# One head group of batch 1 transposed by DMA instead of TensorE

## The chip, the cores and the metric

The kernel runs on one core of a Trainium2 chip. The metric is the device time of one execution in microseconds (us); the time of a kernel is the median of its runs. A profile is one execution recorded instruction by instruction; its span runs from the first to the last instruction.

## What is computed

Attention with squared ReLU in place of a softmax, for 8 batches of 12 heads, 448 positions and head width 64, then a normalized two-layer feed-forward with a residual:

```
scores = q @ k.T / sqrt(64)
attn   = maximum(scores, 0)**2 / 448
x      = heads side by side of (attn @ v)          # 8 x 448 x 768
xn     = (x - mean) / sqrt(var + 1e-6) * g_ln
out    = x + maximum(xn @ w_ch1, 0) @ w_ch2        # 768 -> 3072 -> 768
```

## The kernel before, in words

The order of all work is written out by hand: each engine runs its instructions in the order in which the program emits them, and a helper, `interleave` (L13), deals the units of one list among those of another.

Attention goes by groups. A group is one batch and four heads (two pairs of heads); batch b has the groups 3b, 3b+1 and 3b+2, so group 5 is the third group of batch 1, and groups 6 to 8 belong to batch 2. For each group q, k and v are loaded by POOL's DMA queue with a cast to bf16 (`load`, L108). The scores contract over the head width, so q and k have to be transposed first. Two ways are in the kernel:

- `transposes` (L180): TensorE transposes 14 blocks of q and 14 of k against an identity (L201) into PSUM, and VectorE copies them to SBUF (L208). Used for batches 0 and 1 (`by_dma = 2`, L369).
- `keys_dma` and `queries_dma` (L224, L230): SyncE issues one DMA transpose for the keys (L228) and two for the queries (L233, L234). Used from batch 2 on.

The transposed keys by DMA go to three rotating buffers (`kT`), the transposed queries to two (`qT`). The same two are used by `transposes` for the first group of batch 1. The other groups of batch 1 have their transposes in `hold`, a buffer that also takes the raw q and k of batch 1; later the tile `xtok` lies in the same place.

`scores` (L273) multiplies, applies ReLU on ScalarE (L292) and squares on VectorE; `values` (L300) multiplies with v; `centre` (L349) subtracts the mean. For batches 0 and 1 attention is cut into two blocks of query positions (`attention_block`, L388), and the units of a block are dealt among the units of the first feed-forward product of the block before (`ffn1`, L487): the list at L595 to L611 is

```
interleave(ffn1_units(0, BLK[0][0]), attention_block(0, BLK[0][1]), 3, 1)
... second-layer weights, loads of groups 6 to 8 ...
interleave(ffn1_units(0, BLK[0][1]), attention_block(1, BLK[1][0]), 3, 1)
interleave(ffn1_units(1, BLK[1][0]), attention_block(1, BLK[1][1]), 3, 1)
tokens(0)
```

The transposes of group 5 are a unit of their own in the third of these lines. `tokens` (L463) is one long DMA transpose on SyncE (L467) that brings the attention output of a pair of batches to tokens on partitions; `statistics` (L471) and `roots` (L477) compute the scale of each token from it, and `ffn2` (L525) applies that scale to the second product. The scores of batch 2 and later are dealt among the units of `ffn2`.

On POOL's queue stand, in order: q, k, v of batch 0, the first-layer weights (`load_w1`, 12 DMAs), then q, k, v of group 3, q and k of group 4, q and k of group 5, v of groups 4 and 5 (each behind a product of batch 0), the second-layer weights (`load_w2`, 4 DMAs, L142), and q, k of groups 6, 7 and 8 with v of group 6. A DMA that reuses a buffer waits on that queue until the buffer's last reader is done.

Of the kernel before, what the change touches and what calls it, by code (L numbers as in the profile page):

```python
# [12 lines left out]
def interleave(main, side, free=0, ahead=0):  # L13


    for unit in side[:ahead]:
        unit()
    side = side[ahead:]
    n, done = len(main) - free, 0
    for i, unit in enumerate(main):  # L20
        unit()
        want = min(len(side), (len(side) * (i + 1)) // n)
        while done < want:
            side[done]()
            done += 1
# [3 lines left out]
def kernel(  # L29
# [23 lines left out]
    P = 128  # L53
# [8 lines left out]
    J = S // HP  # L62
    NP = H // 2
    G = NP // 2
# [35 lines left out]
    qkv = {}  # L100
# [5 lines left out]
    groups = [(b, m) for b in range(B) for m in range(G)]  # L106

    def load(n, names):  # L108
        if n >= len(groups):
            return  # L110
        b, m = groups[n]
        for name in names:
            if b == 1 and name != "v":
                o = (2 * m + "qk".index(name)) * 2 * S
                t = hold[:, o:o + 2 * S].rearrange("p (r s) -> p r s", r=2)
            elif name == "q":
                t = qbuf[m][:, D:D + 2 * S].rearrange("p (r s) -> p r s", r=2)
            else:
                t = io.tile([P, 2, S], bf16, tag=name, name=name + "_sb", bufs=4 if name == "v" else 3)
            nc.gpsimd.dma_start(t, srcs[name][b][:, m:NP:G, :])  # L120
            qkv[name, b, m] = t
# [8 lines left out]
    hold = xtpool.tile([P, K1, NT, P], bf16, tag="xtok", name="hold_sb")  # L130
    hold = hold.rearrange("p c t d -> p (c t d)")
# [3 lines left out]
    def load_w1(i):  # L135
        s = slice(i * NCH, (i + 1) * NCH)
        for hf in range(2):
            nc.gpsimd.dma_start(w1[hf * HP:(hf + 1) * HP, :, s], w1_src[hf][:, :, s])  # L138
# [11 lines left out]
    load(2, "v")  # L150
    for i in range(6):
        load_w1(i)
    load(3, "qkv")
    load(4, "qk")
    load(5, "qk")

    ones = const.tile([P, P], bf16)
    nc.vector.memset(ones, 1.0)
# [21 lines left out]
    def transposes(b, m):  # L180


        if b == 0:
            o = 12 * 1024 + m * 2 * J * P
            sb = early[:, o:o + 2 * J * P].rearrange("p (i c) -> p i c", c=P)
        elif m:
            o = (m - 1) * 2 * J * P
            sb = hold[:, o:o + 2 * J * P].rearrange("p (i c) -> p i c", c=P)
        else:
            sb = tpool.tile([P, NB, P], bf16, tag="qT", name="qT_sb")  # L190
        for i, n in enumerate(("q", "k")):
            src = qkv[n, b, m]
            if (b, m) == (0, 0):
                idle((36, 4)[i])
            if b == 0:
                ps = ps_mm.tile([P, 1024], bf16, tag="mm", name="tr_ps")
            else:
                ps = ps_sc.tile([P, 2, 1024], bf16, tag="sc", name="tr_ps")[:, 0]
            for j in range(J):
                for pr in range(2):  # L200
                    nc.tensor.transpose(  # L201
                        ps[pr * HP:(pr + 1) * HP, j * P:(j + 1) * P],
                        src[:, pr, j * D:(j + 1) * D], identity)

            cuts = ((nc.vector.tensor_copy, 0, 3), (nc.scalar.copy, 3, J)) if (b, n) == (0, "k") \
                else ((nc.vector.tensor_copy, 0, J),)
            for copy, lo, hi in cuts:
                copy(sb[:, i * J + lo:i * J + hi, :],  # L208
                     ps[:, lo * P:hi * P].rearrange("p (j c) -> p j c", c=P))
        if (b, m) == (0, 0):  # L210
            idle(3)
        squares_now()
        st[b, m] = {
            "q": lambda i, r: sb[:, 0:J],
            "k": lambda i: sb[:, J + i],
            "where": lambda pr, j: (j, pr),
            "attn": []}
# [6 lines left out]
    def keys_dma(n):  # L224
        if n >= len(groups):
            return
        kts[n] = tpool.tile([P, J, P], bf16, tag="kT", name="kT_sb", bufs=3)
        nc.sync.dma_start_transpose(kts[n], qkv[("k",) + groups[n]].rearrange("p r s -> p (r s)"))  # L228

    def queries_dma(n):  # L230
        m, kt = groups[n][1], kts[n]
        qt = tpool.tile([P, NB, P], bf16, tag="qT", name="qT_sb")
        nc.sync.dma_start_transpose(qt[:, 0:2 * J + 1:2, :], qbuf[m][:, :])  # L233
        nc.sync.dma_start_transpose(qt[:, 1:2 * J:2, :], qbuf[m][:, D:D + 2 * S])  # L234

        def queries(i, r):
            o = (2 * i + r) // J * J + 1 - r
            return qt[:, o:o + J]
        st[groups[n]] = {
            "q": queries,  # L240
            "k": lambda i: kt[:, i],
            "where": lambda pr, j: divmod(pr * J + j, 2),
            "attn": []}
# [122 lines left out]
                xc[b][:, c, of(blk)], total, g_mean[:, c:c + 1], xc[b][:, c, of(blk)],  # L366
                op0=ALU.mult, op1=ALU.add)

    by_dma = 2  # L369

    def transposed(n):

        if groups[n][0] < by_dma:
            transposes(*groups[n])
            return


        if n == by_dma * G:
            keys_dma(n)
        else:  # L380
            if n == by_dma * G + 1:
                load(n + 2, "k")
            load(n + 3, "k")
            load(n + 2, "q")
        queries_dma(n)
        keys_dma(n + 1)

    def attention_block(b, blk):  # L388


        lo, hi, first = b * G, b * G + G, blk[0] == 0
        units = [lambda: transposed(lo)] if first else []

        def unit(n, part):
            squares_now()
            for i in range(4 * part, min(4 * part + 4, J), 2):
                if (b, blk) == FIRST and n == G - 1:
                    busy(1)
                scores(n, tuple(range(i, min(i + 2, J))), blk)
            if b == 1 and not first and part and n == hi - 1:  # L400
                transposed(hi)
            if part and n > lo:
                values(n - 1, blk)
                if not first:
                    load(n + 3, "v")
        for n in range(lo, hi):
            units.append(lambda n=n: unit(n, 0))
            if first and n + 1 < hi:
                units.append(lambda n=n: transposed(n + 1))
            units.append(lambda n=n: unit(n, 1))  # L410

        def last():
            if (b, blk) == FIRST:
                busy(1)
            values(hi - 1, blk)
            if (b, blk) == FIRST:
                busy(2)
            if b == 1 and not first:
                load(hi + 3, "v")
        units.append(last)  # L420
        units.append(lambda: centre(b, blk))
        return units

    def attention(bs):

        lo, hi = bs[0] * G, (bs[-1] + 1) * G
        seq = [(n, i) for n in range(lo, hi) for i in range(J)]

        def item(n, i):
            if i == 0 and n + 1 < len(groups) and groups[n + 1][0] >= by_dma:
                transposed(n + 1)
            scores(n, (i,), FULL)

        def product(n):
            values(n, FULL)  # L440
            load(n + 4, "v")

        def bundle(items, at):
            for o, it in enumerate(items):
                item(*it)
                if o == at:
                    product(it[0] - 1)
        units, due = [], [[], []]
        for s in range(0, len(seq), 3):
            items = seq[s:s + 3]  # L450
            at = max((o for o, (n, i) in enumerate(items[:2]) if n > lo and i in (1, 2)), default=-1)
            units.append(lambda items=items, at=at: bundle(items, at))
            n = items[at][0] - 1
            due.append([groups[n][0]] if at >= 0 and groups[n][1] == G - 1 else [])
            units += [lambda b=b: centre(b, FULL) for b in due.pop(0)]
        units.append(lambda: product(hi - 1))
        units.append(lambda: None)
        return units
# [112 lines left out]
    def ffn1_units(b, blk=FULL):  # L571
        if blk == FULL:
            return [lambda ni=ni: ffn1(b, ni, blk) for ni in range(K2)]
        return [lambda: ffn1_head(b, blk)] + [lambda ni=ni: ffn1(b, ni, blk) for ni in range(3, K2)]
# [20 lines left out]
    pairs = B // 2  # L595
    for unit in attention_block(0, BLK[0][0]):
        unit()
    interleave(ffn1_units(0, BLK[0][0]), attention_block(0, BLK[0][1]), 3, 1)
    w2 = wpool.tile([P, K2, d_model], bf16, tag="w2", name="w2")
    for i in range(4):  # L600
# [52 lines left out]
```

## Time and profile before

| what | value |
|---|---|
| median of three runs | 551.65 us (550.57 to 553.97) |
| profiled execution, its own time | 549.99 us |
| its span | 548.2 us |
| granted TensorE clock | 0.997 |
| PE, DVE, ACT, POOL busy | 539.8, 266.3, 258.5, 110.4 us |
| transposes on TensorE (L201) for batch 1 | 84, from 42.1 to 54.7 us |
| first DMA transpose of keys and queries issued | 73.7 us |
| last second-layer weight DMA issued, landed after | 44.8 us, 26.7 us |

In the lines of the profile PE is TensorE's matmuls, PEld its weight loads, DVE VectorE, ACT ScalarE, POOL GpSimd and SP SyncE; a q behind the name (SPq) is the engine's queue, which issues DMAs. `L201` is line 201 of the kernel. In a timeline a line has the start, the duration, the instruction with what it writes and reads, how many were merged, and in brackets the idle time of the engine before it with what ended it. The row "DMA" of the forty slices gives the busy share of the DMA engines in tenths. Of the DMA queues, q0 (software_dynamic) carries what POOL issues and q1 (hardware_dynamic) what SyncE issues; the columns are packets, megabytes and the time of the packets as a share of the window.

### The profile page before, as it was taken

To read this page: it belongs to the slowest core of one execution; us is meant where nothing else is said; L and a number is where in the kernel's file an instruction comes from. 1 tells how busy PE (TensorE), PEld (TensorE's weight loads), DVE (VectorE), ACT (ScalarE), POOL (GpSimd) and SP (SyncE) were. 2 spreads that over 40 slices of the span, in tenths; PEclk is the share of its full clock that TensorE was granted. 3 is DMA by queue.
4 is the path that set the end of the run, shared out by engine and by line. 5 is a ranking of instruction groups with operands and counts; after the bars stand their busy time and mean duration, and the time that the engine had idled before them with its cause. 6 is when DMAs were issued, how large, how long until landed. Compare 5 with 4: busy or idle time off the path is not lost.

```text
span 548.2 us, 10993 instructions
## 1 busy us (share of the span) xinstructions
PE 539.8 (98%) x4742; PEld 319.0 (58%) x4742; DVE 266.3 (49%) x511; ACT 258.5 (47%) x420; POOL 110.4 (20%) x136
## 2 busy tenths in 40 slices
PE   7999999999999999999999999999999999999997
PEld 6687779755555555555555555555555555556665
DVE  3776753278887250057787532027687680001111
ACT  4676675555543444455545344445545254440000
POOL 8344102024424210002633400001230400000000
PEclk9899999999999999999999999999999999999999
DMA  9999999979994970018999892004941240001222
GB/s 144 206 205 208 211 190 172 111 116 158 148 179 92 155 112 1 0 41 131 159 157 143 108 155 35 0 1 92 169 102 30 59 102 0 1 0 30 59 57 59
DMA packets 107216, 56.16 MB, mean 102 GB/s; under 512 B 77216, under 2 KB 103712, under 8 KB 107168
## 3 DMA queue, kind: packets, MB, share of 16 engines
q0 software_dynamic: 27520, 25.96, 33.3%
q1 hardware_dynamic: 79408, 29.31, 31.8%
q8 instruction: 37, 0.61, 0.5%
q10 hardware_dynamic: 240, 0.20, 0.1%
q14 instruction: 11, 0.09, 0.0%
HBM read 51.91 MB, written 11.01 MB: 115 GB/s over the span
## 4 chain that ended last, share of the span: by engine, by line
PE 92%; DMA 5%; POOL 2%; issue 0%; DVE 0%; POOLq 0%
PE o_ps L533 39%; PE h_ps L495 38%; PE sc_ps L281 6%; PE av_ps L311 5%; DMA w<-in_moe_w_ch_dram 5%; PE o_ps L558 1%; PE h_ps L517 1%; PE sum_ps L359 1%; PE tr_ps L201 0%; POOL v_sb L120 0%; POOL k_sb L120 0%; POOL w L138 0%; POOL q_sb L120 0%; DVE o_sb L561 0%; POOL identity masks.py:199 0%
## 5 line engine op out<-in xcount | busy, mean ns | idle before, releaser
L495 PE MATMUL h_ps<-xc_sb,w 128*128 128x448 bf16 (+2 forms) x1368 | 219.1, 318 | 0.7 <-DVE hT_sb L501 0.4
L533 PE MATMUL o_ps<-w,hT_sb 128*128 128x384 bf16 x1296 | 219.6, 326 | 0.0
L495 PEld LDWEIGHTS <-w 128*128 128x128 bf16 x1368 | 128.6, 98 | 86.9 <-issue 3.2
L533 PEld LDWEIGHTS <-hT_sb 128*128 128x128 bf16 x1296 | 123.1, 98 | 94.3 <-issue 16.1
L292 ACT ACTIVATE attn_sb<-sc_ps 128x896 bf16<-128x896 f32 (+4 forms) x150 | 126.3, 902 | 83.6 <-PE sc_ps L281 83.6
L503 ACT ACTIVATE hT_sb<-h_ps 128x448 bf16<-128x448 f32 (+2 forms) x212 | 102.5, 483 | 121.6 <-PE h_ps L495 121.1
L294 DVE TENSOR_TENSOR attn_sb<-attn_sb 128x896 bf16<-128x896 bf16 x126 | 81.6, 654 | 38.1 <-ACT attn_sb L292 37.1
L539 DVE SCALAR_TENSOR_TENSOR o_sb<-o_ps,rstd_sb,xtok_sb 128x384 f32<-128x384 f32 x54 | 33.0, 611 | 48.5 <-PE o_ps L533 48.5
L480 DVE RECIPROCAL rstd_sb<-rstd_sb 128x1 f32<-128x1 f32 (+1 forms) x10 | 1.7, 168 | 97.5 <-ACT rstd_sb L479 97.5
L342 POOL TENSOR_TENSOR part_sb<-part_sb,xT_sb 128x448 f32<-128x448 f32 x24 | 29.5, 1229 | 70.5 <-DVE xT_sb L318 62.9
L474 DVE BATCH_NORM_STATS2 stats<-xtok_sb 128x6 f32<-128x384 bf16 x56 | 27.5, 533 | 33.3 <-DMA xtok_sb<-xT_sb 33.3
L365 DVE SCALAR_TENSOR_TENSOR xc_sb<-total_sb,g_mean,xc_sb 128x448 bf16<-128x448 f32 (+2 forms) x54 | 29.0, 606 | 21.3 <-ACT total_sb L363 21.3
L339 POOL TENSOR_TENSOR part_sb<-xT_sb 128x448 f32<-128x448 bf16 x6 | 6.6, 1105 | 140.1 <-DVE xT_sb L318 110.3
L281 PE MATMUL sc_ps<-qT_sb,kT_sb 64*64 64x448 bf16 x504 | 34.7, 357 | 0.0
L311 PE MATMUL av_ps<-attn_sb,v_sb 64*64 64x448 bf16 (+2 forms) x672 | 32.3, 327 | 0.0
L318 DVE TENSOR_SCALAR xT_sb<-av_ps 128x896 bf16<-128x896 f32 (+2 forms) x30 | 27.0, 901 | 10.4 <-PE av_ps L311 10.4
L311 PEld LDWEIGHTS <-v_sb 64*64 64x64 bf16 x840 | 23.3, 109 | 11.4 <-issue 2.5
L120 POOL DMA_DIRECT2D k_sb<-in_k_dram x21 | 15.1, 720 | 71.0 <-DMA kT_sb<-k_sb 38.5
L324 DVE TENSOR_SCALAR xc_sb<-xT_sb,g_sb 128x448 bf16<-128x448 bf16 (+2 forms) x58 | 28.8, 546 | 1.0
L120 POOL DMA_DIRECT2D v_sb<-in_v_dram x24 | 17.5, 733 | 21.6 <-PE av_ps L311 17.7
L281 PEld LDWEIGHTS <-kT_sb 64*64 64x64 bf16 x504 | 11.5, 105 | 16.9 <-issue 13.5
L292 ACT ACTIVATE early<-sc_ps 128x768 bf16<-128x768 f32 (+3 forms) x24 | 18.4, 826 | 1.5 <-PE sc_ps L281 1.3
(60 smaller groups left out, 195.6 us busy)
## 6 DMA issues: line engine op xcount, KB each, us to landing
out_dram<-o_sb SPq DMA_DIRECT2D x54, 192.0 KB, 2.9
v_sb<-in_v_dram POOLq DMA_DIRECT2D x24, 224.0 KB, 5.0
q_sb<-in_q_dram POOLq DMA_DIRECT2D x21, 224.0 KB, 7.5
k_sb<-in_k_dram POOLq DMA_DIRECT2D x21, 224.0 KB, 6.7
w<-in_moe_w_ch_dram POOLq DMA_DIRECT2D x12, 384.0 KB, 14.5
w<-in_moe_w_ch_dram POOLq DMA_DIRECT2D x4, 1152.0 KB, 20.0
hold_sb<-in_q_dram POOLq DMA_DIRECT2D x3, 224.0 KB, 11.9
hold_sb<-in_k_dram POOLq DMA_DIRECT2D x3, 224.0 KB, 11.2
```

What stands on the lines that cost most here:

```text
L120: nc.gpsimd.dma_start(t, srcs[name][b][:, m:NP:G, :])
L281: nc.tensor.matmul(ps[cols, r, o * w:(o + 1) * w], g["k"](i)[rows, cols], g["q"](i, r)[rows, blk[0]:sum(blk), cols], start=True, stop=True)
L292: nc.scalar.activation(a, ps[:, :, :len(slots) * w], ACTF.Relu)
L294: nc.vector.tensor_mul(a, a, a)
L311: nc.tensor.matmul(ps[cols, hh, :w], v_sb[rows, pr, j * D:(j + 1) * D], g["attn"][i][rows, r, :], start=(j == 0), stop=(j == J - 1))
L324: nc.vector.tensor_scalar_mul(xc[b][:, c, of(blk)], xT[b // 2][:, c, of(blk, b)], g_sb[:, c:c + 1])
L342: nc.gpsimd.tensor_add(part[b], part[b], x[:, c])
L365: nc.vector.scalar_tensor_tensor(xc[b][:, c, of(blk)], total, g_mean[:, c:c + 1], xc[b][:, c, of(blk)], op0=ALU.mult, op1=ALU.add)
L495: nc.tensor.matmul(ps[:, :w], w1[:, c, ni * P:(ni + 1) * P], xc[b][:, c, of(blk)], start=(c == 0), stop=(c == K1 - 1))
L503: nc.scalar.activation(hT[pair][:, ni, o:o + w], ps[:, :w], ACTF.Relu)
L533: nc.tensor.matmul(ps[:, :DH], hT[pair][:, ki, t * P:(t + 1) * P], w2[:, ki, cols], start=(ki == 0), stop=(ki == K2 - 1))
L539: nc.vector.scalar_tensor_tensor(o_sb[t][:, cols].rearrange("p (c d) -> p c d", d=D), ps[:, :DH].rearrange("p (c d) -> p c d", d=D), rstd[ ...
```

## The change

Group 5 is transposed by DMA. The border between the two ways is now counted in groups (`by_dma = 2 * G - 1`, which is 5, with G = 3 groups in a batch). Raw q of group 5 goes to the query buffer that group 2 used (`qbuf[2]`), raw k to one of the rotating k buffers. The loads of batch 1 are emitted after the first attention block, and those of group 5 stand right behind q and k of group 3, ahead of v of group 3 and q and k of group 4. The three DMA transposes of group 5 are the first on SyncE's queue after two small loads of `g_ln`. The transposed queries of group 5 take the first of the two `qT` buffers, those of group 3 the second; before, group 3 took the first and group 6 the second. `interleave` deals one unit fewer in that stage.

```
-            if b == 1 and name != "v":
+            if b == 1 and m < G - 1 and name != "v":
...
-    load(3, "qkv")
-    load(4, "qk")
-    load(5, "qk")
...
-            o = (m - 1) * 2 * J * P
-            sb = hold[:, o:o + 2 * J * P].rearrange("p (i c) -> p i c", c=P)
+            sb = hold[:, :2 * J * P].rearrange("p (i c) -> p i c", c=P)
...
-    by_dma = 2
+    by_dma = 2 * G - 1

     def transposed(n):
-        if groups[n][0] < by_dma:
+        if n < by_dma:
             transposes(*groups[n])
             return
-        if n == by_dma * G:
+        if n == by_dma:
+            keys_dma(n)
+            queries_dma(n)
+            return
+        if n == by_dma + 1:
             keys_dma(n)
         else:
-            if n == by_dma * G + 1:
+            if n == by_dma + 2:
                 load(n + 2, "k")
...
-            if first and n + 1 < hi:
+            if first and n + 1 < min(hi, by_dma):
                 units.append(lambda n=n: transposed(n + 1))
...
     for unit in attention_block(0, BLK[0][0]):
         unit()
+    load(3, "qk")
+    load(5, "qk")
+    transposed(by_dma)
+    load(3, "v")
+    load(4, "qk")
     interleave(ffn1_units(0, BLK[0][0]), attention_block(0, BLK[0][1]), 3, 1)
```

More of the change, by code (lines that the diff above doesn't have):

```diff
@@ L434, in item @@
         def item(n, i):
-            if i == 0 and n + 1 < len(groups) and groups[n + 1][0] >= by_dma:
+            if i == 0 and n + 1 < len(groups):
                 transposed(n + 1)
```

## The prediction

> **What bounds the kernel now.** I read the totals first, then the forty slices, the chain that ended last, the timeline of TensorE around the removed transposes, SyncE's timeline, the DMA queues by window, and last the moment at which the second pass of the feed-forward starts. The page of before:
>
> ```profile
> PE 539.8 (98%) x4742; PEld 319.0 (58%) x4742; DVE 266.3 (49%) x511; ACT 258.5 (47%) x420; POOL 110.4 (20%) x136
> ...
> DMA  9999999979994970018999892004941240001222
> ...
> PE 92%; DMA 5%; POOL 2%; issue 0%; DVE 0%; POOLq 0%
> ```
>
> TensorE is busy 98% and is 92% of the chain. But the DMA row stands at 9 in eleven of the first twelve slices (164 us) and at 7 in the other: in the stage that the change touches, two things are full, TensorE and the DMA engines. TensorE there (columns: start us, us, instruction):
>
> ```profile
> 52.50 1.48 PE L495 MATMUL h_ps<-xc_sb,w 128*128 128x256 bf16 x12
> 53.91 0.97 PE L201 MATMUL tr_ps<-identity,hold_sb 128*64 128x128 bf16 x28
> 54.82 1.49 PE L495 MATMUL h_ps<-xc_sb,w 128*128 128x256 bf16 x12
> ...
> 58.86 0.63 PE L281 MATMUL sc_ps<-hold_sb 64*64 64x256 bf16 x16
> ```
>
> No row has an idle time: what leaves TensorE here shortens the run, what makes it wait lengthens it. The 28 transposes of group 5 (batch 1, third group) begin at 53.91, the next work at 54.82. The scores of group 5 begin at 58.86. SyncE's DMA transposes and the DMA queues in 73.5 to 77.2 us and 77.2 to 80.6 us:
>
> ```profile
> 73.75 1.30 SPq L228 DMA_TRANSPOSE kT_sb<-k_sb  x1
> 75.16 2.07 SPq L233 DMA_TRANSPOSE qT_sb<-q_sb  x1
> 77.27 3.80 SPq L234 DMA_TRANSPOSE qT_sb<-q_sb  x1
> 81.11 1.30 SPq L228 DMA_TRANSPOSE kT_sb<-k_sb  x1
> 86.32 9.11 SPq L467 DMA_TRANSPOSE xtok_sb<-xT_sb  x1
> ```
> ```profile
> q0 software_dynamic: 887, 0.75, 126.3%
> ```
> ```profile
> q1 hardware_dynamic: 857, 0.22, 88.9%
> q0 software_dynamic: 265, 0.22, 44.4%
> ```
>
> q0 carries POOL's loads, q1 SyncE's transposes. The key transpose issued at 73.75 moved nothing before 77.2; it landed after 7.7 us, at 81.5, the two query transposes at 82.4 and 85.7. The first-pair token transpose (L467), issued at 86.32, landed 19.0 us later, and the second feed-forward product waits for it:
>
> ```profile
> 105.34 1.02 DVE L474 BATCH_NORM_STATS2 stats<-xtok_sb 128x6 f32<-128x384 bf16 x2 [15.24 <-DMA xtok_sb<-xT_sb]
> 106.64 0.29 ACT L479 ACTIVATE rstd_sb<-mv,eps_sb 128x1 f32<-128x1 f32 x1 [4.00 <-DVE mv L475]
> 106.84 2.51 ACT L292 ACTIVATE attn_sb<-sc_ps 128x896 bf16<-128x896 f32 x3
> 109.83 0.76 PE L281 MATMUL sc_ps<-qT_sb,kT_sb 64*64 64x448 bf16 x12
> ```
>
> ScalarE holds the square root and, behind it, the three evictions that free the three score accumulators. They end at 109.35; the third score of the next bundle needs its accumulator at 110.34 (two thirds into the 0.76 us from 109.83). The token transpose may land 1.0 us later than 105.3 before TensorE waits: at 106.3.
>
> **The change part by part.** The sum is made against the profiled execution: span 548.2 us, 549.99 us with what lies around it. The median of the three runs is 551.65, so 1.66 us are added at the end.
>
> *Removed.* 28 transposes with their weight loads: 54.82 - 53.91 = 0.91 us of TensorE, all on the path. Two VectorE copies at 0.616 us (the copy's own row): VectorE idles 1.44 us right after them, so they are worth nothing.
> By the Trainium skill (TensorE: Matmul & The Clock Gate, PE-mode transpose) a transpose costs about 275 ns in a kernel's context; 28 would be 7.7 us and the time 544. The row speaks against it: 28 in 0.91 us are 33 ns each, although each lasts 219 ns, so they overlap, and I keep the row.
>
> *Order on TensorE.* One unit fewer is spread among the feed-forward units, so the transposes of group 4 come one unit (0.71 us) later, 48.46 instead of 47.75, and the scores of group 5 one unit and 0.91 us earlier, at 57.2. The work is the same: nothing.
>
> *POOL's queue.* q and k of group 5 load ahead of v of group 3 and q, k of group 4. The loads land one every 1.1 us, in order. So q5 lands at 42.2 and k5 at 43.4 (the places of v3 and q4 before), v3 moves to 44.6, q4 to 45.6, k4 to 46.8. Group 4 needs q4 at 48.5 and k4 half a microsecond later: 2 us of margin; v3 is needed at 56. The new waits are on buffers: q5 on the transposes of group 2 (over at 13.3 us), and the loads q8 and k8 on the new transposes. Those two loads were held by weight landings until 60.5 and 66.2; behind them on POOL stand v loads that wait for TensorE until 78.3. Nothing, unless the new transposes land after 60.
>
> *Added on SyncE's queue.* Three DMA transposes from 43.5 us on. SyncE waited until 73.75 anyway, so the issue is free. Their landing is not: TensorE needs all three at 57.2. Nearest row: the same three at 73.75, also behind a full q0, landed 7.7, 8.6 and 11.9 us after the first issue. That gives 51.2, 52.1 and 55.4: 1.8 us to spare, price nothing. The difference: there q0 had two loads left after the first packet of q1, here it has the four second-layer weight loads (1152 KB, one landing every 5.6 us, from 49 to 71.5). Lower end 0 (the transposes cannot bring a gain), upper end the rivals below.
>
> *What they take from the loads.* Alone, q1 moves 0.28 MB in the microsecond from 83 to 84, so the three (0.72 MB) need 2.6 us of all DMA engines; mixed, both queues together fell from 208 GB/s (60 to 73.5 us) to 136 (77.25 to 80.75). I take 2.6 to 5 us of delay for all loads behind. The last weight load then lands at 74 to 76.5 (needed at 101), k6 at 76 to 79, k7 at 80 to 82.
>
> *The query buffers.* Two rotate. Group 5 now takes one, so the query transposes of group 6 must wait until group 5's last scores have read it: 82.3 - 0.9 = 81.4 us instead of 75.16. Behind that wait on SyncE stand the second query transpose, the keys of group 7 and the token transpose. Their issue took 2.07 + 3.80 + 1.30 us, with gaps 7.3, when the queue was full; the same three took 1.32 + 1.48 + 1.89 later (115.29 to 120.13). SyncE is free at 86.2 to 88.7; the token transpose's data is ready at 85.4. Keys of group 7 landed 5.3 us after issue (81.11), so at 89.5 to 92.5 instead of 86.4, and the token transpose, whose first packets came at 89.5, starts 0 to 3 us later. It lands at 105.3 to 108.3; I take 106.9, the middle, since neither row is nearer. Against the 106.3 that cost nothing this is +0.6: the 0.91 gained is waited away and 0.6 more. Ends: -0.9 and +2.0. Group 6's own scores need their transposes at 105 and have them by 92; group 7's, behind the token transpose, are needed at 113.6 and landed at 108.5, so 3 us more is free.
>
> Sum: -0.91 + 1.5 (TensorE's wait at the token statistics) = +0.6: profiled 550.6, median 552.3. All later stages keep their work.
>
> **The rivals.** *A, no new wait.* The token transpose lands by 105.4, and only the 0.91 is seen: 549.1 profiled, 550.7 median. For it: from 86.4 to 89.5 q1 was empty, and the later group could use that gap. Against it: SyncE's issue of the token transpose alone took 9.11 us, so the queue is choked as it is.
>
> *B, the transposes take turns with whole weight loads; slower.* In 77.2 to 80.6 the queues mixed, but nobody shows how long one turn of q0 is with 1152 KB loads. If the second and third transpose each wait for one weight load, the third starts when the second load ends: 60.2 + 2.5 = 62.7, lands about 64.5 with its own 0.8 and a tail of 1. TensorE waits 64.5 - 57.2 = 7.3, less 0.9: +6.4, so 558. It decides once the third lands after 58.1; with one weight load in between it lands near 58 to 59 and costs about nothing net.
> The Trainium skill (DMA: Bandwidth & Descriptors, Queues, rings and completion order) has each DMA engine alternate between queues packet by packet, with up to 64 descriptors in a packet. No run here shows the packet of a weight load; the rule is what would make B's turns long and C impossible.
>
> *C, the transposes starve until q0 runs dry; slower.* For it: q1's first packet at 77.2, when q0's rate fell. Against it: in 149.5 to 152.5 q1 moved 0.33 MB beside 0.30 of q0, with loads still waiting. Price: POOL stops at q8, whose buffer the transposes hold, so q0 ends with k7 at 77.1; the transposes end 2.6 to 4.9 later, at 79.7 to 82. TensorE waits 22 to 25: near 574.
>
> *D, the change doesn't take place:* the instruction order has 28 fewer transposes on TensorE and three more on SyncE, so it does.
>
> **How the numbers follow.** What the measurement can tell from no change is about 1%, 5.5 us. Forecast (a wait at the token statistics, -0.5 to +2.5 net): 0.53. A: 0.22. B: 0.15, of it 0.06 within 5.5 us. C: 0.08. Faster by over 1% has no mechanism in the rows: 0.02. So faster 0.02, same 0.53 + 0.22 + 0.06 = 0.81, slower 0.09 + 0.08 = 0.17. The predicted time is the forecast's, 552.3. The range goes from A less a microsecond of scatter of the medians (three runs lay between 550.57 and 553.97), 549.7, to B, 558.5; it leaves out C and the tails, 0.12 in all.
>
> **What would show it.** In the profile after: 28 rows of L201's group fewer and 0.91 us less before the scores of group 5; the first key transpose issued near 43.5 and the three landings before 57 (B: about 64; C: about 80, with a hole in TensorE there); the first query transpose of group 6 issued at 81 to 82; the token transpose landing at 106 to 108 and an idle time of TensorE of 0.5 to 2 us at the first scores after 109. I am wrong if TensorE waits at group 5's scores, or if q4 and k4 land after 48.5.

## The result, and the profile after

| | before | after |
|---|---|---|
| median | 551.25 us (550.51 to 553.97, 6 runs) | 569.53 us (568.33 to 571.11, 6 runs) |
| ratio to before | | 1.0317, interval 1.0292 to 1.0342 |
| profiled execution: own time, span | 549.99, 548.2 us | 569.36, 567.2 us |
| granted clock, mean | 0.997 | 0.984 |

The forecast was 552.3 us in a range from 549.7 to 558.5. The kernel became 3.2% slower. The page of after, the same lines as were shown of before and one group of instructions:

```profile
PE 538.9 (95%) x4714; PEld 318.4 (56%) x4714; DVE 265.2 (47%) x509; ACT 258.7 (46%) x420; POOL 110.6 (19%) x136
...
PEclk9999679999999999999999999999999999999999
DMA  9999994895999594003999597004743150001222
...
PE 91%; DMA 5%; DVE 1%; POOL 1%; issue 0%; ACT 0%; SPq 0%; POOLq 0%
...
L277 PE MATMUL sc_ps<-qT_sb,kT_sb 64*64 64x448 bf16 (+2 forms) x560 | 37.3, 352 | 17.3 <-DMA qT_sb<-q_sb 17.3
```

TensorE works 0.9 us less (538.9 instead of 539.8), as intended, but the span is 19.0 us longer. The group of the scores has 17.3 us of idle time in front of it, all of it ended by the DMA `qT_sb<-q_sb`. The clock row falls to 6 and 7 in the fifth and sixth slice (56.7 to 85 us). The timeline of TensorE in after:

```profile
56.73 1.48 PE L495 MATMUL h_ps<-xc_sb,w 128*128 128x256 bf16 x12
75.53 1.06 PE L277 MATMUL sc_ps<-qT_sb,kT_sb 64*64 64x256 bf16 x16 [17.31 <-DMA qT_sb<-q_sb]
76.53 2.34 PE L495 MATMUL h_ps<-xc_sb,w 128*128 128x256 bf16 x12
78.80 0.52 PE L277 MATMUL sc_ps<-qT_sb,kT_sb 64*64 64x256 bf16 x12
```

One hole, at the first scores of group 5. SyncE's timeline shows what it waited for:

```profile
44.15 1.31 SPq L224 DMA_TRANSPOSE kT_sb<-k_sb  x1
45.58 8.53 SPq L229 DMA_TRANSPOSE qT_sb<-q_sb  x1
54.15 7.82 SPq L230 DMA_TRANSPOSE qT_sb<-q_sb  x1
...
91.14 1.23 SPq L229 DMA_TRANSPOSE qT_sb<-q_sb  x1
...
105.00 8.50 SPq L467 DMA_TRANSPOSE xtok_sb<-xT_sb  x1
```

The first three are group 5's. They were issued 0.65 us later than the prediction said (44.15 instead of 43.5), and landed at 58.1, 67.3 and 75.4 us, not at 51.2, 52.1 and 55.4. The four second-layer weight loads landed at 58.5, 65.2, 72.1 and 78.1 (before: 54.6, 60.2, 65.9, 71.5). What both queues moved, by the DMA view: before in 60 to 66 us, then after in 60 to 66 us, then after in 60 to 60.143 us (queue: packets, MB, share of the window):

```profile
q0 software_dynamic: 835, 1.26, 116.0%
```
```profile
q0 software_dynamic: 688, 1.03, 94.0%
q1 hardware_dynamic: 688, 0.18, 22.0%
```
```profile
q0 software_dynamic: 16, 0.02, 93.7%
q1 hardware_dynamic: 16, 0.00, 21.7%
```

A packet of the trace is one row: 1536 bytes of a weight load, 256 bytes of a transpose. In six microseconds of after, the two queues moved exactly as many rows as each other. In 143 ns they moved 16 of each, and a weight row takes 134 ns of that (93.7% of 143): each of the 16 DMA engines does one row of the one queue and one of the other, in turn. So a transpose advances one short row for each long one: 688 in 6 us, 115 per us. From the three, 896 + 1024 + 896 = 2816 rows come; at that rate they need 24.5 us. Their first row is seen 4.0 us after the issue, at 48.15; 48.15 + 24.5 = 72.7, and for 1.5 us near 53 neither queue moved much: 74.2, where 75.4 was measured. Alone, the same rows go at 1123 per us (before, 83 to 84 us), ten times as fast.

The second feed-forward product started at 120.79 instead of 102.11, 18.68 us later: 0.80 that this execution already had at 42 us (it waited longer for its first loads), -0.91 for the transposes, +17.31 for the wait, +1.29 for slower matmuls behind it, +0.17 at one wait for VectorE. That is 18.66. At the token statistics, where the prediction put its loss, TensorE does not wait in after: everything there is 18 us late anyhow.

### The profile page after: what moved, and what is told of

The parts are those of the page before. It is cut to its first block, busy times and chain, and to the rows that moved or that the text cites. A ratio compares the mean times of both kernels' runs of the same rounds, so it can differ in the third digit from the quotient of the medians.

```text
span 567.2 us, 10941 instructions
## 1 busy us (share of the span) xinstructions
PE 538.9 (95%) x4714; PEld 318.4 (56%) x4714; DVE 265.2 (47%) x509; ACT 258.7 (46%) x420; POOL 110.6 (19%) x136
## 4 chain that ended last, share of the span: by engine, by line
PE 91%; DMA 5%; DVE 1%; POOL 1%; issue 0%; ACT 0%; SPq 0%; POOLq 0%
PE o_ps L533 38%; PE h_ps L495 37%; PE sc_ps L277 7%; PE av_ps L307 6%; DMA qT_sb<-q_sb 4%; DMA k_sb<-in_k_dram 1%; PE o_ps L558 1%; PE h_ps L517 1%; PE sum_ps L355 1%; PE tr_ps L197 0%; POOL q_sb L120 0%; DVE early L266 0%; POOL k_sb L120 0%; PE busy_ps L253 0%; DVE xT_sb L314 0%
## 5 line engine op out<-in xcount | busy, mean ns | idle before, releaser
L277 PE MATMUL sc_ps<-qT_sb,kT_sb 64*64 64x448 bf16 (+2 forms) x560 | 37.3, 352 | 17.3 <-DMA qT_sb<-q_sb 17.3
L361 DVE SCALAR_TENSOR_TENSOR xc_sb<-total_sb,g_mean,xc_sb 128x448 bf16<-128x448 f32 (+2 forms) x54 | 29.0, 606 | 21.4 <-ACT total_sb L359 21.4
L277 PEld LDWEIGHTS <-kT_sb 64*64 64x64 bf16 x560 | 12.9, 107 | 35.2 <-issue 31.8
L501 DVE TENSOR_SCALAR hT_sb<-h_ps 128x192 bf16<-128x192 f32 (+1 forms) x16 | 6.2, 390 | 31.4 <-PE h_ps L495 30.9
```

Source lines behind the costliest of these rows:

```text
L277: nc.tensor.matmul(ps[cols, r, o * w:(o + 1) * w], g["k"](i)[rows, cols], g["q"](i, r)[rows, blk[0]:sum(blk), cols], start=True, stop=True)
L361: nc.vector.scalar_tensor_tensor(xc[b][:, c, of(blk)], total, g_mean[:, c:c + 1], xc[b][:, c, of(blk)], op0=ALU.mult, op1=ALU.add)
```

## The experiments

The theory: the queues alternate **row by row**, so the long rows of the weights set the pace of the transposes. The first rival (B of the prediction): turns of whole loads. Two more: the transposes get a fixed share of the bytes, whatever the rows, or SyncE's slow issue of a transpose is the cause. A second question came up on the way: what the transposes cost the other loads, if nobody waits for them. "3rd" is the landing of group 5's third transpose, "token" that of the first token transpose (before: 105.3; after: 75.4 and 122.6).

| run | median, us | ratio to its own before, interval | 3rd | idle at group 5's scores | token |
|---|---|---|---|---|---|
| e1, weights in 8 DMAs | 569.11 | 1.0319 (1.0273 to 1.0365) | 73.8 | 16.82 | 119.8 |
| e2, weights in 24 DMAs | 568.63 | 1.0294 (1.0256 to 1.0333) | 72.2 | 14.61 | 119.5 |
| e5, rows of 768 bytes | 559.87 | 1.0153 (1.0137 to 1.0168) | 64.4 | 7.01 | 112.0 |
| e10, old order of loads | 571.77 | 1.0351 (1.0302 to 1.0400) | 77.1 | 19.92 | 127.1 |
| e3, weights held back | 555.55 | 1.0065 (1.0034 to 1.0097) | 53.3 | 0 | 109.1 |
| e6, spare transposes | 558.20 | 1.0121 (1.0105 to 1.0137) | 75.4 | 0 | 110.7 |
| e7, held, loads of 6 and 7 first | 559.62 | 1.0139 (1.0111 to 1.0168) | 53.1 | 0 | 116.0 |
| e8, as e7, query buffer free | 562.56 | 1.0192 (1.0161 to 1.0222) | 53.7 | 0 | 115.8 |
| e9, seven transposes ahead of the weights | 558.38 | 1.0108 (1.0065 to 1.0150) | 57.2 | 0 | 110.9 |
| e11, no transposes of group 5 | 552.07 | 0.9983 (0.9952 to 1.0013) | none | 0 | 107.2 |
| e12, TensorE kept busy, 125 | 569.71 | 1.0307 (1.0262 to 1.0353) | 74.9 | 10.81 | 122.2 |
| e13, TensorE kept busy, 300 | 569.48 | 1.0326 (1.0302 to 1.0350) | 76.2 | 0.21 | 123.3 |
| e4, unused transposes | 584.19 | 1.0584 (1.0550 to 1.0617) | 75.6 | (31.09) | 137.4 |

### e1 and e2: whole loads, or rows?

```
-    for i in range(4):
-        load_w2(w2, i, 4)
+    for i in range(8):          # e2: 24
+        load_w2(w2, i, 8)       # e2: 24
```

> The second-layer weights load in 8 DMAs of 576 KB instead of 4 of 1152 KB; nothing else differs from the kernel after. Turns (my theory now): each DMA transpose waits for the end of one whole weight load of the other queue, so the step between the three landings follows the size of a load. It was 9.2 and 8.1 us with a load of 5.6 us; with 2.8 us I expect about 5 to 6 us, the third landing near 63 to 66 us instead of 75.4, TensorE's wait at group 5's scores 5 to 8 us instead of 17.3, the time 554 to 559. Share by volume (rival): the queue of the transposes gets a fixed small share of the DMA engines as long as the loads are queued, whatever their size; then the third lands near 75 and the time stays at 569. Issue (rival): SyncE's own issue of a transpose (8.5 and 7.8 us) is what is slow; the time stays at 569.

> The same with 24 DMAs of 192 KB, each 0.93 us of the DMA engines. Turns: the step between landings is 1.5 to 3.5 us, all three are there by 52 to 57 us, TensorE does not wait at 58 us, and what is left is the gain of the removed transposes and at most a small wait at the token statistics: 549.5 to 552.5. Share by volume and issue: 569 as before.

The timelines of TensorE, of e1 and of e2:

```profile
73.97 1.07 PE L277 MATMUL sc_ps<-qT_sb,kT_sb 64*64 64x256 bf16 x16 [16.82 <-DMA qT_sb<-q_sb]
```
```profile
72.38 1.07 PE L277 MATMUL sc_ps<-qT_sb,kT_sb 64*64 64x256 bf16 x16 [14.61 <-DMA qT_sb<-q_sb]
```

Loads of half and of a sixth of the size leave the wait nearly as it was; turns of whole loads would have shortened it in about the same proportion. That rival, which was the expectation of both runs, is refuted. The 2.7 us that e2 gains here it loses at 164 and 295 us, in two waits of 1.5 and 1.2 us for later query transposes.

### e5: shorter rows

Each of the four weight loads becomes two, one for each half of its columns, so a row has 768 bytes. There are 8 DMAs, as in e1, of the same size.

```
-        nc.gpsimd.dma_start(w2[:, s, :], w2_src[:, s, :])
+        for h in range(2):
+            c = slice(h * DH, (h + 1) * DH)
+            nc.gpsimd.dma_start(w2[:, s, c], w2_src[:, s, c])
```

> The runs with 8 and 24 weight loads refuted the turns of whole loads: the landings stayed 8 to 9 us apart. The packets of the kernel after suggest something finer: from 60 to 66 us the loads' queue moved 688 packets and the transposes' queue 688. Row by row (my theory now): each DMA engine takes one row from either queue in turn, a weight row of 1536 bytes against a row of 256 bytes of a transpose. Here each weight load is cut in two halves of its columns: 8 DMAs of 576 KB as in the run with 8, but rows of 768 bytes. A pair of rows then takes about 83 instead of 143 ns of an engine (rows alone: 117 ns at 1536 bytes, 67 at 896, so about 57 at 768, and 26 for the transpose's row), so the 2816 rows of the three transposes need some 14.6 instead of 25 us: third landing near 63 to 65 us, TensorE's wait 4 to 7 us, time 555 to 559. Share of the bytes (rival): what the transposes get is set by the volume in the other queue; the volume is the same, so the third lands near 74 and the time is 568 to 570, as with 8 DMAs of long rows.

The DMA queues of e5 in 52 to 60 us, TensorE, and SyncE's issue of the two query transposes:

```profile
q0 software_dynamic: 1364, 1.03, 91.2%
q1 hardware_dynamic: 1365, 0.33, 40.9%
```
```profile
64.55 1.07 PE L279 MATMUL sc_ps<-qT_sb,kT_sb 64*64 64x256 bf16 x16 [7.01 <-DMA qT_sb<-q_sb]
```
```profile
44.89 4.61 SPq L231 DMA_TRANSPOSE qT_sb<-q_sb  x1
49.54 5.28 SPq L232 DMA_TRANSPOSE qT_sb<-q_sb  x1
```

Again one for one, now 171 of each per us, and the third transpose lands at 64.4. With the number and the size of the DMAs as in e1, halving the row took 9.8 us off the wait. Row by row is confirmed, by a change of nothing but the row. A share by bytes would have left the landing near 74. The issue times fall with the weights' rows, from 8.53 and 7.82 us to 4.61 and 5.28, with nothing changed on SyncE: the slow issue follows from the full queue and is not the cause. Wait and landing are as expected (4 to 7 us, 63 to 65); the median, 559.87, lies 0.9 us above the expected range.

### e10: the order of the loads

q and k of group 5 load where they did before the change, and their transposes are issued there.

```
-    load(3, "qk")
-    load(5, "qk")
-    transposed(by_dma)
-    load(3, "v")
-    load(4, "qk")
+    load(3, "qkv")
+    load(4, "qk")
+    load(5, "qk")
+    transposed(by_dma)
```

> The kernel after with one part undone: the loads stand in the old order (v of group 3 and q, k of group 4 ahead of group 5). k of group 5 lands 3.3 us later. Row by row: the transposes then have fewer short loads beside them and start 3 us later, third landing near 78 to 79, TensorE's wait 20 to 21, time 571 to 574; the order of the loads was worth some 3 us. Rival: the order does not matter because the weights are what the transposes share with; 569 to 570.

```profile
77.27 1.07 PE L277 MATMUL sc_ps<-qT_sb,kT_sb 64*64 64x256 bf16 x16 [19.92 <-DMA qT_sb<-q_sb]
```

The key transpose is issued 3.0 us later (47.15) and lands 2.5 us later. The second half of the change, the order of the loads, shortens the wait by 2.6 us (19.92 to 17.31); the medians point the same way, but their intervals overlap. The loss comes from the first half.

### e3: the weights wait for the transposes

POOL copies one column of each of the three transposed tiles before it issues the weight loads, so they cannot mix.

```
+    seen = spool.tile([P, 3], bf16, tag="seen", name="seen", bufs=1)
+    for i, t in enumerate((kts[by_dma][:, 0, :1], qt5[0][:, 0, :1], qt5[0][:, 1, :1])):
+        nc.gpsimd.tensor_copy(seen[:, i:i + 1], t)
     for i in range(4):
         load_w2(w2, i, 4)
```

> The weights stay in 4 DMAs of 1152 KB, but POOL reads one column of each transposed tile just ahead of them, so that they are issued when the three transposes of group 5 have landed. Turns: beside the transposes only the v loads of groups 4 and 5 (1.1 us each) are under way, so the third lands near 52 to 55 us and TensorE does not wait there; the weights follow some 8 to 12 us late, still by 85 us, before they are needed at 101. 549.5 to 553, the upper part if the token transpose is late, as my prediction had it (idle time of TensorE after the first scores past 109 us). Share by volume: nothing else is queued either, so the same; issue: the transposes still take 8 us each to issue and the time is 560 or more.

The transposes land at 50.3, 52.6 and 53.3, and there is no wait at group 5. What is left, in the timelines of ScalarE and of TensorE of e3:

```profile
110.43 0.29 ACT L481 ACTIVATE rstd_sb<-mv,eps_sb 128x1 f32<-128x1 f32 x1 [8.54 <-DVE mv L477]
110.64 2.51 ACT L290 ACTIVATE attn_sb<-sc_ps 128x896 bf16<-128x896 f32 x3
```
```profile
111.58 0.38 PE L279 MATMUL sc_ps<-qT_sb,kT_sb 64*64 64x448 bf16 x4 [2.43 <-ACT attn_sb L290]
112.39 0.38 PE L279 MATMUL sc_ps<-qT_sb,kT_sb 64*64 64x448 bf16 x4 [0.42 <-ACT attn_sb L290]
113.20 0.59 PE L279 MATMUL sc_ps<-qT_sb,kT_sb 64*64 64x448 bf16 x4 [0.42 <-ACT attn_sb L290]
```

This is the wait at the token statistics that the prediction named. The weights, held until 53.8, landed at 80.4 at the latest, k of group 6 behind them at 82.6 instead of 73.7, and the token transpose at 109.1 instead of 105.3; the square root on ScalarE stands ahead of the evictions, and TensorE waits 3.27 us for them. The prediction's bound, no cost up to 106.3, gives 109.1 - 106.3 = 2.8. The expected time, 549.5 to 553, was missed (555.55): the scores after the wait go at the pace of ScalarE's evictions, and the 18 products behind them take 4.50 us instead of 3.10.

### e4 and e6: the traffic alone

Both keep the transposes on TensorE and add three DMA transposes that nobody reads. e4 is the kernel after with that edit; there the TensorE transposes stand behind the load of q of group 8 into the same buffer.

> TensorE transposes group 5 as in the kernel before, and the three DMA transposes are issued as in the kernel after, into buffers that nobody reads. All else of the change stays (order of the loads, place of the raw q and k, rotation of the query buffers). If the wait at group 5's scores is the whole loss, this takes the time of before, 549 to 553, though the third transpose still lands near 75 and the weights up to 7 us late. If the delay of the other loads costs by itself, it is slower than that by as much.

```profile
84.76 0.96 PE L197 MATMUL tr_ps<-identity,q_sb 128*64 128x128 bf16 x14 [31.09 <-DMA q_sb<-in_q_dram]
```

TensorE waits 31 us for q of group 8 and transposes that in place of group 5's: a wait of the edit's own making, which tells nothing about the traffic. e6 is built on the kernel before, with the new order of the loads:

```
+    load(3, "qk")
+    load(5, "qk")
+    nc.sync.dma_start_transpose(spare_k, hold[:, o5 + 2 * S:o5 + 4 * S])
+    nc.sync.dma_start_transpose(spare_q[:, 0:2 * J + 1:2, :], hold[:, o5:o5 + 2 * S + 2 * D])
+    nc.sync.dma_start_transpose(spare_q[:, 1:2 * J:2, :], hold[:, o5:o5 + 2 * S])
+    load(3, "v")
+    load(4, "qk")
```

> The kernel before with one thing added: loads in the order of the kernel after, and three DMA transposes of group 5's raw keys and queries into buffers that nobody reads, issued where the kernel after issues them. TensorE still transposes group 5. If the wait at group 5's scores is the whole loss, this takes 550 to 553 (the loads behind come 4 to 7 us late, and the token transpose perhaps 1 us), although the third transpose still lands near 73 to 75. If the mixed traffic costs by itself, this shows it, up to 569.

The expectation failed: 558.2, 1.2% slower, without any wait at group 5. TensorE of e6, and its granted clock (window; the column before the last two):

```profile
113.19 0.59 PE L278 MATMUL sc_ps<-qT_sb,kT_sb 64*64 64x448 bf16 x4 [3.05 <-ACT attn_sb L289]
...
115.33 5.16 PE L530 MATMUL o_ps<-w,hT_sb 128*128 128x384 bf16 x18
```
```profile
115.30:118.00 2.70, 2.70 (x13) 1.33 (x10) 2.34 (x6) 2.06 (x3) 0.75 (x2) 0.50 0.77 93
118.00:120.40 2.40, 2.40 (x11) 1.06 (x9) 1.68 (x5) 0.00 (x0) 0.00 (x0) 0.68 0.82 147
```

The weights land up to 79.4 (before 71.5), and k of group 6 at 81.1, so SyncE's keys of group 6 go out at 81.1 instead of 73.7, the token transpose at 94.2 instead of 86.3, and it lands 5.4 us later, at 110.7. The next 24 products of the second product's list start 6.9 us later (121.11 instead of 114.25): 0.25 from ahead of the wait, 3.05 of idle time, 1.45 because the next scores go at the pace of ScalarE's evictions, and 2.06 because the 18 products behind take 5.16 us instead of 3.10 at a clock of 0.50 to 0.68; together 6.8. The three transposes delay the loads by 7 to 8 us even if nobody reads them, and the token transpose behind those loads has a margin of 1.

### e7, e8 and e9: is there an order without the cost?

e7 is e3 with the loads of groups 6 and 7 ahead of the weights. e8 also keeps group 3's transposed q and k in `hold`, so a query buffer is free earlier. e9 goes furthest: seven transposes (group 5's, group 6's and the keys of group 7) land before POOL issues the weights.

```
# e7
-    for i in range(4):
-        load_w2(w2, i, 4)
-    load(6, "qkv")
-    load(7, "qk")
+    (e3's three copies)
+    load(6, "qkv")
+    load(7, "qk")
+    for i in range(4):
+        load_w2(w2, i, 4)
# e8 and e9
-            sb = tpool.tile([P, NB, P], bf16, tag="qT", name="qT_sb")
+            sb = hold[:, 4 * J * P:6 * J * P].rearrange("p (i c) -> p i c", c=P)
# e9, ahead of the weights
+    load(6, "qk")
+    load(7, "k")
+    keys_dma(6)
+    queries_dma(6)
+    keys_dma(7)
+    (a copy of one column of each of the seven)
```

> As the run with the weights held until the transposes of group 5 have landed, but q, k, v of group 6 and q, k of group 7 are loaded ahead of the weights. In that run k of group 6 landed at 82.6 and the token transpose was issued at 94.1 and landed at 109.1, 3 us too late. Here the loads land by 60, so that only the query buffer (free at 81.4) holds SyncE: token transpose issued at 86 to 89, landing at 105.5 to 108: time 550 to 553.

> As the run before, and the TensorE transposes of group 3 are kept in the part of hold that raw q and k of group 5 no longer need, so that only DMA transposes use the two query buffers: the transposes of group 6 wait for nothing but their loads. Row by row they share the engines with the weights and land by 85, the weights by 90, both in time (105 and 101). The token transpose is issued when its data is ready, as before, and lands by 105.4. What is left of the change is the 0.9 us of TensorE: 549.5 to 551.5, the best of all if the wait at the token statistics was the second cost, as predicted. If it isn't that wait, this equals the run before.

> Row by row says: keep the DMA transposes and the weight loads apart. Here q, k of group 6 and k of group 7 load right after the v loads of group 5, the DMA transposes of groups 5 and 6 and the keys of group 7 follow at once, POOL issues the four weight loads when all seven have landed, and group 3's TensorE transposes lie in hold so that the query buffers are free. I expect the seven landed by 60 to 63, the weights by 86 (needed at 101), the token transpose issued when its data is ready and landed by 106, no wait of TensorE at group 5's scores: 549.5 to 552, not distinguishable from the kernel before by more than 0.3%. If the loss of the earlier runs came from something else than mixing (the volume of the DMA transposes by itself, rival), this stays at 555 or more.

All three missed. In e7 and e8 group 6's transposes meet the weights, now later, and the token transpose lands at 116. e7 also shows which buffer group 6's query transposes wait for, because their loads were there by 58.5. Group 3's scores read `qT_sb` alone, group 5's read `qT_sb` and `kT_sb`; TensorE and SyncE of e7:

```profile
71.42 0.44 PE L279 MATMUL sc_ps<-qT_sb 64*64 64x192 bf16 x12
...
81.34 0.44 PE L279 MATMUL sc_ps<-qT_sb,kT_sb 64*64 64x192 bf16 x12
```
```profile
71.91 1.23 SPq L230 DMA_TRANSPOSE qT_sb<-q_sb  x1
```

They go out when group 3's last scores end (71.86), ten microseconds ahead of group 5's. The buffer was not held until 81.4, as e7's expectation and the prediction had it. In e8, where group 3 has no part in the query buffers, they go out at 61.8, right behind the keys. In e9 the seven landed by 62.5, as expected, the weights from 72.2 to 90.2; SyncE and then TensorE of e9:

```profile
85.85 21.42 SPq L469 DMA_TRANSPOSE xtok_sb<-xT_sb  x1
```
```profile
113.38 0.59 PE L279 MATMUL sc_ps<-qT_sb,kT_sb 64*64 64x448 bf16 x4 [3.96 <-ACT attn_sb L290]
```

The token transpose now goes out early, but beside the last weight load and the ten loads behind it, which land from 92.3 to 106.9, and its issue alone takes 21.4 us. In all three orders the token transpose, or the transposes ahead of it, share full engines with the weights and the loads behind them. These three orders do not exhaust what could be tried.

### e11: what the removal is worth

Neither TensorE nor a DMA transposes group 5, and its scores are computed from group 4's tiles.

```
+        if n == 5:
+            squares_now()
+            st[groups[5]] = dict(st[groups[4]], attn=[])
+            return
```

> The kernel before without the transposes of group 5 and without any DMA in their place; the scores of group 5 use the transposed tiles of group 4, so the output of that group is another one. This is the gain that the change could have at best: 28 transposes, 0.91 us, so 550.0 to 550.9 where before has 551.3 (ratio 0.998). If it is more (rival: the copies on VectorE or the score accumulators held TensorE too), 549.5 or less.

The ratio is 0.9983, from 0.9952 to 1.0013: it agrees with 0.91 us in 551 (0.9983), and cannot be told from nothing. Were the DMA transposes free, this is what the change could gain.

### e12 and e13: the slower matmuls behind the wait

Matmuls of a tile of ones, read by nobody, stand ahead of group 5's first scores: 125, then 300.

```
+        if n == by_dma and slots[0] == 0 and blk == BLK[1][0]:
+            warm = ps_mm.tile([P, 512], fp32, tag="mm", name="warm_ps")
+            for _ in range(125):          # e13: 300
+                nc.tensor.matmul(warm[:, :P], ones, ones, start=True, stop=True)
```

> The kernel after with 125 matmuls of ones by ones in front of group 5's scores, about 14 us of the 17 that TensorE waits there; nobody reads them. In the kernel after, the granted clock fell after the wait (slices 5 and 6 of the page at 0.6 and 0.7 to 0.9), and the first 28 matmuls after it took 1.3 us longer than in the kernel before. If that is the clock, they take their normal time here, and the whole is 1.0 to 1.5 us faster than after (568 to 568.6, mean clock 0.99 or more). If those matmuls were slow for another reason (rival), the time stays at 569.5.

> The kernel after, with 300 matmuls of ones by ones ahead of the first scores of group 5, instead of 125: at 57 ns each they take 17.1 us and fill nearly all of the 17.3 us of waiting, so under 1 us of idle time is left. If the 1.29 us that the work behind the wait lost (scores 1.06 instead of 0.63 us, the next product 2.34 instead of 1.48) came from the lower granted clock after an idle TensorE, the clock stays at 1.00 from 70 to 80 us, the scores take 0.6 and the product 1.5, and the time is 1 to 1.5 us below the kernel after: ratio to before 1.029 to 1.030, 568 to 568.5. If it came from something else near the wait (full DMA queues at that moment, the scores' own buffers), the scores still take about 1.06 and the product 2.3, and the time is that of the kernel after, 1.031.

The 125 took only 7.1 us, 10.81 us of idle time remained, and the scores still took 1.07 us: inconclusive. Of after, the window table of the wait and what follows it (the granted clock is the column before the last two), then TensorE and the same windows of e13:

```profile
58.00:66.00 8.00, 0.22 (x2) 0.00 (x0) 0.99 (x3) 0.38 (x1) 0.72 (x1) 0.70 1.16 201
...
72.00:75.00 3.00, 0.00 (x0) 0.00 (x0) 0.00 (x0) 0.00 (x0) 0.00 (x0) 0.50 1.18 204
75.00:76.50 1.50, 0.97 (x16) 0.63 (x16) 0.00 (x0) 0.28 (x1) 0.54 (x1) 0.50 1.20 206
76.50:79.00 2.50, 2.50 (x24) 1.75 (x24) 0.97 (x3) 1.75 (x3) 0.89 (x2) 0.64 1.25 203
79.00:84.00 5.00, 4.83 (x92) 3.72 (x85) 3.84 (x10) 2.90 (x6) 0.00 (x0) 1.00 1.33 203
```
```profile
59.18 16.91 PE L274 MATMUL warm_ps<-ones 128*128 128x128 bf16 x300
76.30 0.63 PE L281 MATMUL sc_ps<-qT_sb,kT_sb 64*64 64x256 bf16 x16 [0.21 <-DMA qT_sb<-q_sb]
76.86 1.48 PE L499 MATMUL h_ps<-xc_sb,w 128*128 128x256 bf16 x12
```
```profile
75.00:76.50 1.50, 1.29 (x28) 1.15 (x29) 0.00 (x0) 0.00 (x0) 0.00 (x0) 1.00 1.21 214
76.50:79.00 2.50, 2.50 (x52) 1.85 (x47) 1.27 (x3) 2.24 (x4) 1.43 (x2) 1.00 1.23 203
```

With the wait filled, the clock stays at 1.00 and the scores take 0.63 instead of 1.06 us, the product 1.48 instead of 2.34, beside DMA engines just as full. So in after the 1.29 us come from the lowered clock. But the expected gain of 1 to 1.5 us is not seen: the median did not fall (569.48 against 569.53). The profiled execution of e13 was 1.1 us later already at the last product before the wait, and it has a pause of 1.11 us on TensorE at 120.9 that ends by nothing the profile shows. Whether that pause belongs to the edit stays open.

## Why the prediction was wrong, point by point

- **Added on SyncE's queue: this step failed.** It took the three landings from the row at 73.75 (7.7, 8.6 and 11.9 us after the first issue) and priced TensorE's wait at nothing. Measured were 13.9, 23.2 and 31.2 us, and a wait of 17.3 us, the prediction's own sign of being wrong. It named the difference itself, two loads left on q0 there and four weight loads here, and did not work it out. In the lines that it shows, q0 moved 265 rows from 77.2 to 80.6 and q1 857: the loads ran out, and most rows of the transposes went alone. In after, q0 had rows for all of the time: from 48.15 to 75.4 it moved 3045 packets beside 2912 of q1, so all 2816 rows went at the weights' pace, 24.5 us. The slow start was not the error. Beside loads, a transpose's first row came 3.6 to 4.0 us after its issue at 73.75 in before and at the first transpose of after, e1, e3, e6 and e10, and with no loads 1.2 us after it (after, 91.14).
- **B, turns with whole weight loads** had the right place (TensorE waits at group 5's scores, the weights loading meanwhile) and the wrong mechanism and size: e1 and e2 rule out whole loads; the wait is 17.3 us instead of 7.3. The Trainium skill (DMA: Bandwidth & Descriptors, Queues, rings and completion order) has the engines change between queues packet by packet, 9 to 17 descriptors typically in a packet. The alternation agrees with the trace; the length does not, since here each engine changes after every row (16 and 16 in 143 ns), and the measurement decides.
- **C, starving until q0 runs dry,** is refuted: q1 moved 688 rows in the 6 us in which q0 moved 688. Of the 148 packets of q1 that the prediction set against it (149.5 to 152.5 us), 106 are over 2 KB, so they are no transposes; the alternation in after is the better argument. C was nearest in size (574) by luck, with a mechanism that the trace does not show.
- **Removed** was right: TensorE is busy 0.9 us less, and e11's median does not speak against it.
- **Order on TensorE and POOL's queue** were right: q5, k5, v3, q4 and k4 landed at 43.0, 44.1, 45.5, 46.4 and 47.5, each 0.7 to 0.9 us behind the forecast, as this execution was from 42 us on; group 4's transposes did not wait, and TensorE was ready for group 5's scores at 58.2 (forecast 57.2).
- **What they take from the loads** was too small: the last weight landed 6.6 us later, 5.8 without the 0.8 of this execution, instead of 2.6 to 5.
- **The query buffers,** the step that carried the forecast, was wrong about the buffer. Group 6's query transposes wait for group 3's last scores, not for group 5's: they go out at 71.9 in e7, not at 81.4, and in after at 91.1, when group 3's last scores (90.65 and 0.44) end. 71.9 is ahead of the 73.75 at which SyncE could begin in before, so this wait alone would have cost nothing. What put SyncE back in e3 and e6 was the load of k of group 6, which landed at 82.6 and 81.1 behind the delayed weights. The rest of the step held: a token transpose past 106.3 made TensorE wait, in e3 (109.1, 3.27 us) and in e6 (110.7, 3.05 us at the first of the scores). Its size was short of what lies behind such a wait: slower scores and a lowered clock, another 3.5 us in e6.

## What to carry to other kernels

Where two DMA queues are full at the same time, count rows and not bytes: a transfer of short rows beside one of long rows advanced here at the pace of the long ones, so its duration, as long as the other queue has rows, is its number of rows divided by the other queue's rows per microsecond. Before work is moved from TensorE to DMA, look whether the DMA row is at 9 in that stage; there, as e6 shows, the loads behind a transpose pay for it, even if nobody waits for the transpose. A landing time is to be taken from a row whose neighbours on the other queue have the same row size and last as long.

## What the runs showed of the hardware that was not expected

- The strict alternation, one row each: 16 and 16 in 143 ns with rows of 1536 bytes, 1364 and 1365 in 8 us with rows of 768.
- SyncE is held while it issues a DMA transpose into a backlog: 1.2 us at best, 8.5 us behind the first transpose in after; the long token transpose 9.1 us in before and 21.4 us in e9. What stands behind it on the queue is late by as much.
- The first row of a DMA transpose came 1.2 us after its issue with no load beside it (after, 91.14), and 3.6 to 4.0 us after it beside loads, at the first transposes of before, after, e1, e3, e6 and e10.
- In the 17 us of idle time of after the granted clock fell to 0.50, and it was at 1.00 again by 79 us; TensorE's work behind the wait took 1.29 us more for it. The Trainium skill (TensorE: Matmul & The Clock Gate, Part 1) has the clock at half after about 3.4 us without work and back after about as long of sustained work. The windows of after agree roughly: 0.70 on average from 58 to 66 us puts the fall near 61.2, 3.0 us after the last work, and 0.64 from 76.5 to 79 puts the rise near 78.3, 2.8 us after work began. In e13, with the wait filled, it did not fall. In e6 it stood at 0.50 in the windows behind an idle time of 3.05 us, a little less than the page's length.
